# Splitting TensorE products: 64-row pairs in two streams, or one 128-row instruction with 64-row pairs where they remain

## The chip, the cores and the metric

The kernel runs on one core of one Trainium2 chip. The metric is the device time of one execution in microseconds (us), taken over several runs. The profiled execution is one run of the same program with the hardware profiler on; its instruction times are what the views of the profile show.

Engines are named as in the profile: PE is TensorE (PEld is its weight load), DVE is VectorE, ACT is ScalarE, POOL is GpSimd, SP is the engine that issues most transfers.

## What is computed

There are 33,280 tokens (8 batches of 4,160) of 192 features. A short causal convolution with 7 taps comes first, whose weights are a softmax per token and head (8 heads of 24 features); then a layer that takes the largest of three linear maps to 768 hidden features, and one linear map back to 192:

```python
w = softmax(weight_gen, axis=-1)                      # b, s, 8 heads, 7 taps
x = einsum("bshk,bskhg->bshg", w, windows_of(x_pad))  # 33280 x 192
h = maximum(maximum(x @ w1, x @ w2), x @ w3)          # 33280 x 768
out = h @ w_out                                       # 33280 x 192
```

The kernel computes h as x @ w1 plus the larger of zero, x @ (w2 - w1) and x @ (w3 - w1). The x @ w1 @ w_out part needs no hidden layer at all: w1 @ w_out is composed once into a 192 x 192 matrix (tiles `wca` and `wcb`). So there are two hidden products for each of 768 hidden features, `i` = 0 and 1.

Every product is made in the format F32R, and float32 accuracy is reached by splitting each operand into a high part (rounded to F32R) and a low part (the rest): hi·hi + lo·hi + hi·lo.

## The kernel before, in words

The tokens are cut into 65 chunks (`c`) of 512 tokens, each of 4 blocks (`t`) of 128. For each chunk:

- `taps` multiplies by the 7 taps on POOL (line 370, one instruction per block) and sums on DVE (line 382).
- `blocks` turns the result so that features lie on partitions: for the first two chunks on PE (lines 402 and 403), afterwards by a transpose on DVE (line 421) and 24 small copies on ACT (line 432). 192 features are 128 (`a`) and 64 more (`b`).
- `parts` makes the splits: `xa_hi` (ACT, line 444) and `xa_lo` (line 460) of the 128, and of the last 64 the tiles `xc` (the hi, on both halves of the 128 rows, line 449) and `xb` (the lo, on one half of the rows, line 465).
- `up` (line 826) makes the hidden products of one group of 128 hidden features (`j` = 0 to 5) and one `i`, into one of 8 PSUM banks; `SLOT[512]` is the planner's cost of one. ACT then takes the ReLU of `i` = 0 (line 859), DVE the maximum with `i` = 1 (line 867), ACT rounds to `h_hi` (line 871), and DVE or, for `j` = 1 and 4, POOL makes `h_lo` (line 878).
- `down` (line 887) makes the output of one block from `h_hi`, `h_lo`, the chunk's split features, `wo` (hi and lo of w_out beside each other, 2 x 192 columns) and `wca`, `wcb`. ACT and DVE add the two halves of the columns (lines 928 and 935), and SP stores.

All products go through `products` (line 792, the matmul itself is line 802). It makes each product as two instructions of 64 rows: the lower half of the rows ("L") and the upper half ("U"), which are two tiles of the array. The two halves of one product sum into the same bank, so the upper half's first instruction waits until the lower half's last has ended; an instruction of SP that does nothing (line 808) carries that wait. While the upper half of one bank runs, the lower half of the next one does. Of one bank of `up`, the halves hold 4 or 5 products each: `xa_hi`·`wa_hi`, `xa_lo`·`wa_hi`, (`xb` or `xc`)·`wb_hi`, `xa_hi`·`wa_lo`, and in the half named `odd` also `xc`·`wb_lo`. So one `up` is 9 instructions of 64 rows and 512 columns. One `down` is 15 of each half: per half 7 or 8 of 384 columns and 8 or 7 of 192.

Per chunk these are 12 x 9 + 4 x 30 = 228 instructions of 64 rows.

The order of the instructions on each engine is found ahead of the run by a planner (class `Plan`): every piece of work is a task with a cost, an engine, its predecessors, a due time, and the buffers that it holds. The lists "L" and "U" are kept in the order in which the program adds them; the other engines take, of what is ready in the plan, the task with the earliest due time. The order in which tasks start in the plan is the order in which they are emitted. In the list of PE, the four `down` of chunk c - 1 stand in chunk c before `j` = `DOWN_AT` = 3.

Between the `up` of chunk 0 and chunk 1, `turn_weights` (lines 731 and 733) transposes w1 on PE: for each j one F32 transpose of 128 rows and two of 64 rows. `compose` (line 750) then makes `wca` and `wcb` by F32 products on all 128 rows.

Of the kernel before, what the change touches and what calls it, by code (L numbers as in the profile page):

```python
# [10 lines left out]
F32 = mybir.dt.float32  # L11
# [29 lines left out]
class Plan:  # L41
# [3 lines left out]
    FIXED = ("L", "U")  # L45
    LATENCY = 0.12

    def __init__(self, pools):
        self.free = dict(pools)
        self.waiting = {"L": [], "U": []}  # L50
        self.tasks = []
# [79 lines left out]
def lightconv_maxout_kernel(  # L131
# [30 lines left out]
    DOWN_AT = 3  # L162
# [71 lines left out]
    def hold(name):  # L234
        return Hold(name)
# [7 lines left out]
    def pin(ins):  # L243
        tc.keep_in_program_order(ins)
        return ins
# [4 lines left out]
    def act(n):  # L250
        return 0.18 + 0.00084 * n
# [138 lines left out]
    def blocks(c, ha, sums, wait):  # L390
# [3 lines left out]
        if c < ON_TENSOR:  # L394
            ba, bb = hold("bank"), hold("bank")
            got = []
            for t in range(TC):
                to = slice(t * P, (t + 1) * P)

                def turn(t=t, to=to):  # L400
                    acc = buf(ha)
                    pin(nc.tensor.transpose(buf(ba)[:, to], acc[:, t, :P], ident))
                    pin(nc.tensor.transpose(buf(bb)[:DB, to], acc[:, t, P:], ident))

                got.append(plan.add("L", 0.6, turn, [sums[t], *wait], due, [ba, bb, ha], end=0.9))
            return [ba, bb], lambda: (buf(ba), buf(bb)[:DB]), got
# [30 lines left out]
    def parts(c, hs, places, got):  # L437
# [18 lines left out]
        near = halves[0] if c < ON_TENSOR else halves[low]  # L456
# [6 lines left out]
        def b_low():  # L463
            pin(
                eng.tensor_tensor(  # L465
                    buf(b)[halves[low]], places()[1], buf(k)[near].bitcast(F32), op=ALU.subtract
                )
            )
# [255 lines left out]
    def turn_weights(j):  # L724
# [10 lines left out]
        got = plan.add("L", 0.5, turn, [one_a[jp], one_b[jp], made, *u_last()], 0, [hb], end=0.8)  # L735
# [6 lines left out]
    def compose():  # L742
        for n, (to, at) in enumerate(((wca, 0), (wcb, P))):
# [12 lines left out]
            got = plan.add("L", 2.4, mult, deps + u_last(), 0, [hb, hw1t], end=2.8)  # L756
# [19 lines left out]
    SLOT = {CH: (0.2275, 0.386), 2 * D: (0.166, 0.358), D: (0.12, 0.247)}  # L776
    uppers = []
    last_upper = []

    def u_last():  # L780
        return last_upper[-1:]

    def after(ins, other):
        tc.add_manual_dep(
            ins.ins,
            other.ins.name,
            mybir.DependencyInfo(mybir.DependencyClass.Sync, mybir.DependencyReason.DATA),
            reason="the two halves of the rows don't write to a bank together",
        )
        return ins  # L790

    def products(hb, terms_of):

        begun, before = {}, []
        for half in range(2):
            h = halves[half]
            terms = terms_of(half)
            for q, (n, w, v, deps, holds) in enumerate(terms):
                first, last = q == 0, q == len(terms) - 1

                def emit(n=n, w=w, v=v, h=h, half=half, first=first, last=last):
                    ins = nc.tensor.matmul(  # L802
                        buf(hb)[:, :n], w()[h], v()[h],
                        start=half == 0 and first, stop=half == 1 and last,
                    )
                    pin(ins)
                    if half == 0 and last:
                        begun[0] = pin(after(nc.sync.nop(), ins))
                    elif half == 1 and first:
                        after(ins, begun[0])  # L810

                slot, end = SLOT[n]
                t = plan.add(
                    "LU"[half], slot, emit, [*deps, *(before if first else [])], 0,
                    [hb, *holds], end=end,
                )
            if half == 0:
                before = [plan.add("SYNC", 0.0, lambda: None, [t], 0, [], end=0.3)]
            else:
                last_upper.append(t)  # L820
        return t
# [4 lines left out]
    def up(c, j, i):  # L826
        jp, odd = divmod(j, 2)
        (ah, al, b, k), (hi, lo, bl, cs) = parts_of[c]
        low = 1 - c % 2
        hb = hold("bank")  # L830

        def terms(half):
            got = [
                (CH, lambda: wa_hi[:, j, i], lambda: buf(ah), [w_hi[jp, i], hi], [ah]),
                (CH, lambda: wa_hi[:, j, i], lambda: buf(al), [w_hi[jp, i], lo], [al]),
                (
                    (CH, lambda: wb_hi[:, j, i], lambda: buf(b), [*b_hi[j], bl], [b])
                    if half == low
                    else (CH, lambda: wb_hi[:, j, i], lambda: buf(k), [*b_hi[j], *cs], [k])
                ),  # L840
                (CH, lambda: wa_lo[:, j, i], lambda: buf(ah), [w_lo[jp, i], hi], [ah]),
            ]
            if half == odd:
                got.append((CH, lambda: wb_lo[:, jp, i], lambda: buf(k), [b_lo[jp], *cs], [k]))
            return got

        made = products(hb, terms)
        clock[0] += 4.5 * SLOT[CH][0]
# [38 lines left out]
    def down(c, t):  # L887
# [7 lines left out]
        def terms(half):  # L895
            got = [
                (2 * D, lambda: buf(ah)[:, sl], lambda: wca, first, [ah]),
                (D, lambda: buf(al)[:, sl], lambda: wca[:, :D], first, [al]),
                (
                    (D, lambda: buf(b)[:, sl], lambda: wcb[:, :D], first, [b])  # L900
                    if half == low
                    else (2 * D, lambda: buf(k)[:, sl], lambda: wcb, first, [k])
                ),
            ]
            for j in range(NJ):
                got.append(
                    (
                        2 * D, lambda j=j: buf(hh)[:, j, sl], lambda j=j: wo[:, j],
                        [his[j], o_hi[j], o_lo[j]], [hh],
                    )  # L910
                )
                got.append(
                    (
                        D, lambda j=j: buf(hl)[:, j, sl], lambda j=j: wo[:, j, :D],
                        [los[j]], [hl],
                    )
                )
            return got

        made = products(hb, terms)  # L920
        clock[0] += 7 * (SLOT[2 * D][0] + SLOT[D][0]) + 0.14
# [52 lines left out]
    for c in range(ON_TENSOR, NC):  # L974
        pass
    for c in range(NC):
        if c < ON_TENSOR:
            tokens(c)
        for j in range(NJ):
            if c > 0 and j == DOWN_AT and c < NC - 1:  # L980
# [4 lines left out]
            for i in range(NI):  # L985
                up(c, j, i)
# [45 lines left out]
```

## Time and profile before

| | us |
|---|---|
| median of 3 runs | 1443.07 |
| lowest, highest | 1436.2, 1443.39 |
| the profiled execution, its own time | 1444.6 |
| its span (first to last instruction) | 1442.8 |
| PE busy | 1402.0 |
| ACT, POOL, DVE busy | 1117.3, 1104.2, 1043.4 |
| mean granted clock of PE | 0.987 |

The span is what the views of the profile divide up. A matmul's row has its start and its modelled end: matmuls are pipelined, and neighbours overlap. So the pace is read from the starts, not from the lengths. In the timeline, neighbouring instructions of one kind are merged in one row with their count (x2), from the first one's start to the last one's end. A shape such as 64*128 64x512 is the weights' rows and columns, then the rows and columns of what streams past them.

### The profile page before, as it was taken

The page shows a single profiled execution, that of the slowest core. Times are in us where ns is not written, and L with a number is a line of the kernel's source. Part 1 is how long each engine was busy: PE and PEld are TensorE (multiplying, and loading weights), DVE is VectorE, ACT ScalarE, POOL GpSimd, SP SyncE. Part 2 cuts the span into 40 slices and gives each one's busy share as a digit, 9 for nine tenths or more (in the row PEclk, how much of TensorE's full clock was granted, in tenths as well). Part 3 has the DMA queues.
Part 4 walks back from the last instruction along what each step waited for, and adds up shares of the span by engine and source line. Part 5 has one row for each costly group of instructions (what it writes and reads, how often), then busy time and mean ns, then how long its engine had stood idle before and what let it go on. Part 6 is the DMA issues. An engine that isn't in the chain of part 4 may idle for free.

```text
span 1442.8 us, 37119 instructions
## 1 busy us (share of the span) xinstructions
PE 1402.0 (97%) x14878; PEld 1366.1 (95%) x14878; DVE 1043.4 (72%) x1433; ACT 1117.3 (77%) x2828; POOL 1104.2 (77%) x609
## 2 busy tenths in 40 slices
PE   2889999999999999999999999999999999999999
PEld 1579999999999999999999999999999999999998
DVE  7867777777777787777778777877877677777543
ACT  3547878878877887787788778877888887788773
POOL 6769888778877887887788778778877877787421
PEclk9679999999999999999999999999999999999999
DMA  7102111111111111111011111101111111110000
GB/s 249 46 1 79 57 68 57 68 68 57 68 46 46 57 68 68 68 57 64 28 57 68 68 68 57 68 25 67 57 68 68 57 68 44 48 57 24 23 21 26
DMA packets 23405, 85.08 MB, mean 59 GB/s; under 512 B 2768, under 2 KB 9544, under 8 KB 19136
## 3 DMA queue, kind: packets, MB, share of 16 engines
q1 hardware_dynamic: 23112, 82.44, 15.5%
q8 instruction: 116, 1.90, 0.5%
q14 instruction: 57, 0.47, 0.1%
q10 hardware_dynamic: 120, 0.28, 0.1%
HBM read 57.15 MB, written 25.56 MB: 57 GB/s over the span
## 4 chain that ended last, share of the span: by engine, by line
PE 95%; POOL 1%; DMA 1%; ACT 1%; SPq 1%; DVE 1%; issue 0%; POOLq 0%
PE bank L802 95%; POOL r L370 1%; DMA xt<-in_x_dram 1%; SPq L532 1%; DVE den L344 0%; ACT room L432 0%; DMA raw<-in_moe_w_dram 0%; SPq L516 0%; PE bank L733 0%; ACT m L859 0%; POOL wa_lo L643 0%; PE bank L731 0%; ACT wb_hi L684 0%; DVE acc L382 0%; ACT bank L573 0%
## 5 line engine op out<-in xcount | busy, mean ns | idle before, releaser
L370 POOL TENSOR_TENSOR r<-xt,wt 128x1344 f32<-128x1344 f32 x260 | 727.1, 2845 | 143.2 <-DVE acc L382 142.9
L802 PE MATMUL bank<-wo,h_hi 64*128 64x384 f32 x3120 | 675.0, 357 | 0.0
L802 PE MATMUL bank<-wo,h_lo 64*128 64x192 f32 x3120 | 603.4, 249 | 0.0
L432 ACT COPY room<-room 32x128 f32<-32x128 f32 x1512 | 448.4, 297 | 79.0 <-DVE room L421 55.9
L802 PEld LDWEIGHTS bank<-wo,h_lo 64*128 64x128 f32 x3120 | 493.0, 188 | 0.0
L802 PEld LDWEIGHTS bank<-wo,h_hi 64*128 64x128 f32 x3120 | 489.2, 186 | 0.0
L802 PE MATMUL bank<-xa_hi,wa_hi 64*128 64x512 f32 x1560 | 479.9, 394 | 6.0 <-ACT wa_hi L637 3.4
L802 PE MATMUL bank<-xa_hi,wa_lo 64*128 64x512 f32 x1560 | 477.9, 390 | 3.4 <-POOL wa_lo L643 3.3
L802 PE MATMUL bank<-xa_lo,wa_hi 64*128 64x512 f32 x1560 | 476.8, 391 | 0.5 <-DVE xa_lo L460 0.5
L382 DVE TENSOR_REDUCE acc<-r 128x192 f32<-128x1344 f32 x260 | 399.8, 1538 | 0.6 <-POOL r L370 0.3
L859 ACT ACTIVATE m<-bank 128x512 f32<-128x512 f32 x390 | 234.5, 601 | 71.4 <-PE bank L802 66.7
L935 DVE TENSOR_TENSOR o<-bank,ob 128x192 f32<-128x192 f32 x260 | 92.4, 356 | 268.7 <-ACT ob L928 268.5
L802 PE MATMUL bank<-xb,wb_hi 64*128 64x512 f32 x780 | 284.5, 390 | 0.3 <-DVE xb L465 0.3
L802 PE MATMUL bank<-xc,wb_hi 64*128 64x512 f32 x780 | 281.1, 390 | 0.2 <-ACT wb_hi L684 0.2
L802 PEld LDWEIGHTS bank<-xa_hi,wa_hi 64*128 64x128 f32 x1560 | 255.3, 186 | 13.5 <-ACT wa_hi L637 4.3
L802 PEld LDWEIGHTS bank<-xa_hi,wa_lo 64*128 64x128 f32 x1560 | 255.3, 186 | 11.2 <-POOL wa_lo L643 5.6
L802 PEld LDWEIGHTS bank<-xa_lo,wa_hi 64*128 64x128 f32 x1560 | 254.9, 187 | 6.4 <-DVE xa_lo L460 1.5
L802 PE MATMUL bank<-xc,wb_lo 64*128 64x512 f32 x780 | 258.0, 389 | 0.0
L867 DVE TENSOR_TENSOR bank<-bank,m 128x512 f32<-128x512 f32 x260 | 179.0, 689 | 42.2 <-PE bank L802 24.3
L878 POOL TENSOR_TENSOR h_lo<-m,h_hi 128x512 fp32r<-128x512 f32 x130 | 171.7, 1321 | 40.0 <-ACT h_hi L871 39.9
L802 PE MATMUL bank<-wca,xa_hi 64*128 64x384 f32 x520 | 183.4, 353 | 0.0
L878 DVE TENSOR_TENSOR h_lo<-bank,h_hi 128x512 fp32r<-128x512 f32 x260 | 172.4, 681 | 11.4 <-ACT h_hi L871 11.2
(79 smaller groups left out, 2012.5 us busy)
## 6 DMA issues: line engine op xcount, KB each, us to landing
xt<-in_x_dram SPq DMA_DIRECT2D x31, 1344.0 KB, 5.8
out_dram<-o SPq DMA_DIRECT2D x64, 384.0 KB, 2.3
wt<-in_weight_gen_dram SPq DMA_DIRECT2D x32, 224.0 KB, 2.6
h_hi<-in_moe_w_dram SPq DMA_DIRECT2D x6, 256.0 KB, 2.9
xt<-in_x_dram SPq DMA_DIRECT2D x1, 1152.0 KB, 5.8
h_lo<-in_moe_w_dram SPq DMA_DIRECT2D x6, 128.0 KB, 4.0
raw<-in_moe_w_dram SPq DMA_DIRECT2D x3, 256.0 KB, 3.6
room<-in_moe_w_out_dram SPq DMA_DIRECT2D x2, 384.0 KB, 6.4
```

The source lines that it names most:

```text
L370: nc.gpsimd.tensor_tensor(buf(hr).rearrange("p (h g) k -> p k h g", g=G), buf(hx)[:, la + t : la + t + K].rearrange("p k (h g) -> p k h g" ...
L382: pin(nc.vector.tensor_reduce(buf(ha)[:, t], buf(hr), axis=AX.X, op=ALU.add))
L432: pin(nc.scalar.copy(to[:, :, p : p + 32], b[p : p + 32, :, f : f + 32]))
L532: nc.sync.dma_start(out=raw_b()[h, jps[0] : jps[-1] + 1, i].rearrange("p j n w -> p j (n w)"), in_=w[P:].rearrange("p (j o n) -> p j o n", ...
L802: ins = nc.tensor.matmul(buf(hb)[:, :n], w()[h], v()[h], start=half == 0 and first, stop=half == 1 and last,)
L859: lambda: pin(nc.scalar.activation(buf(hm), buf(hb), AF.Relu)), [made], due,
L867: lambda: pin(nc.vector.tensor_tensor(buf(keep), buf(hb), buf(hm), op=ALU.max)),
L878: eng.tensor_tensor(buf(hl)[:, j], buf(keep), buf(hh)[:, j].bitcast(F32), op=ALU.subtract)
L935: nc.vector.tensor_tensor(buf(ho)[:, t], buf(hb)[:, :D], buf(hq), op=ALU.add)
```

## The change

All products whose operands lie on 128 rows become one instruction of 128 rows. The two lists "L" and "U" become one, "T", in one order, and the instructions on SP that carried the wait from half to half are gone.

- **The splits of the last 64 features.** `xb` now holds the lo on one half of the rows and the hi on the other, so `xb`·`wb_hi` on 128 rows gives both lo·hi and hi·hi. `xc` holds the hi on the half in which `xb` has the lo. The copies are as many as before and as large; one of the two goes to `xb`.
- **`up`** is now called for a pair of groups (`jp`, hidden groups 2jp and 2jp + 1), with four banks. For each bank 4 instructions of 128 rows and 512 columns (`up_full`), and for each `i` one pair of 64 rows (`up_half`): hi·`wb_lo`, the even group on the lower half of the rows and the odd group on the upper half, into two banks. The order in a pair of groups: `up_full` for the two banks of `i` = 0, `up_half` for `i` = 0, `up_half` for `i` = 1 (which begins the two banks of `i` = 1), `up_full` for the two banks of `i` = 1.
- **`down`** is one list of 16 products for each block: 7 of 384 and 9 of 192 columns. All are on 128 rows but the fourth, hi of the last features with the low part of `wcb`, which is one instruction of 64 rows and 192 columns.
- The four `down` of chunk c - 1 stand ahead of pair 1 of chunk c (`DOWN_AT` = 1 of 3), so after 2 groups of 6 and not after 3.
- The planner's costs: one of 512 columns 0.2165 (0.2275 before), of 384 columns 0.163 (0.166), of 192 columns 0.114 (0.12), a pair of `up_half` 0.228.

Per chunk these are 12 x 4 + 6 x 2 + 4 x 16 = 124 instructions on PE.

```diff
-    FIXED = ("L", "U")
+    FIXED = ("T",)
...
-    DOWN_AT = 3
+    DOWN_AT = 1
...
             plan.add(
-                "ACT", act(CH), lambda h=h: pin(nc.scalar.copy(buf(k)[h], places()[1])), of_b,
-                due - 2.5, [k, *hs],
-            )
-            for h in halves
+                "ACT", act(CH),
+                lambda odd=odd: pin(
+                    nc.scalar.copy(buf(k if odd == low else b)[halves[odd]], places()[1])
+                ),
+                of_b, due - 2.5, [k if odd == low else b, *hs],
+            )
+            for odd in range(2)
...
-        bl = plan.add(name, cost, b_low, cs, due - 1.4, [b, k, *hs])
+        bl = [plan.add(name, cost, b_low, cs, due - 1.4, [b, k, *hs]), *cs]
...
-    SLOT = {CH: (0.2275, 0.386), 2 * D: (0.166, 0.358), D: (0.12, 0.247)}
+    SLOT = {CH: (0.2165, 0.386), 2 * D: (0.163, 0.358), D: (0.114, 0.247)}
...
-                    ins = nc.tensor.matmul(
-                        buf(hb)[:, :n], w()[h], v()[h],
-                        start=half == 0 and first, stop=half == 1 and last,
-                    )
-                    pin(ins)
-                    if half == 0 and last:
-                        begun[0] = pin(after(nc.sync.nop(), ins))
-                    elif half == 1 and first:
-                        after(ins, begun[0])
...
+    def product_of(hb, n, w, v, deps, holds, first, last):
+        def emit():
+            pin(nc.tensor.matmul(buf(hb)[:, :n], w(), v(), start=first, stop=last))
+
+        slot, end = SLOT[n]
+        t = plan.add("T", slot, emit, deps, 0, [hb, *holds], end=end)
+        last_product[:] = [t]
         return t
...
+    def up_full(c, j, i, hb, first, last):
+        jp = j // 2
+        (ah, al, b, k), (hi, lo, bl, cs) = parts_of[c]
+        terms = [
+            (lambda: wa_hi[:, j, i], lambda: buf(ah), [w_hi[jp, i], hi], ah),
+            (lambda: wa_hi[:, j, i], lambda: buf(al), [w_hi[jp, i], lo], al),
+            (lambda: wb_hi[:, j, i], lambda: buf(b), [*b_hi[j], *bl], b),
+            (lambda: wa_lo[:, j, i], lambda: buf(ah), [w_lo[jp, i], hi], ah),
+        ]
+        for q, (w, v, deps, h) in enumerate(terms):
+            t = product_of(hb, CH, w, v, deps, [h], first and q == 0, last and q == 3)
...
+    def up_half(c, jp, i, banks, first):
...
+            for odd, h in enumerate(halves):
+                pin(
+                    nc.tensor.matmul(
+                        buf(banks[odd]), wb_lo[h, jp, i], buf(k if odd == low else b)[h],
+                        start=first, stop=not first,
+                    )
+                )
+
+        t = plan.add("T", 0.228, emit, [b_lo[jp], *cs], 0, [*banks, b, k], end=0.42)
...
+    def up(c, jp):
+        banks = {(odd, i): hold("bank") for i in range(NI) for odd in range(2)}
+        of = lambda i: [banks[0, i], banks[1, i]]
+        for odd in range(2):
+            up_full(c, 2 * jp + odd, 0, banks[odd, 0], True, False)
+        t = up_half(c, jp, 0, of(0), False)
+        for odd in range(2):
+            rest(c, 2 * jp + odd, 0, banks[odd, 0], t)
+        up_half(c, jp, 1, of(1), True)
+        for odd in range(2):
+            t = up_full(c, 2 * jp + odd, 1, banks[odd, 1], False, True)
+            rest(c, 2 * jp + odd, 1, banks[odd, 1], t)
...
+        near = halves[1 - low]
+        terms = [
+            (2 * D, lambda: buf(ah)[:, sl], lambda: wca, first, [ah]),
+            (D, lambda: buf(al)[:, sl], lambda: wca[:, :D], first, [al]),
+            (D, lambda: buf(b)[:, sl], lambda: wcb[:, :D], first, [b]),
+            (D, lambda: buf(b)[near, sl], lambda: wcb[near, D:], first, [b]),
+        ]
+        for j in range(NJ):
...
+        for q, (n, w, v, deps, holds) in enumerate(terms):
+            made = product_of(hb, n, w, v, deps, holds, q == 0, q == len(terms) - 1)
```

`rest` is what followed the products in `up` before (ReLU, maximum, `h_hi`, `h_lo`), unchanged.

More of the change, by code (lines that the diff above doesn't have):

```diff
@@ L455, in parts @@
         eng = nc.vector if c < ON_TENSOR else nc.gpsimd
-        near = halves[0] if c < ON_TENSOR else halves[low]
+        near = 0 if c < ON_TENSOR else low
         def a_low():
@@ L465, in b_low @@
                 eng.tensor_tensor(
-                    buf(b)[halves[low]], places()[1], buf(k)[near].bitcast(F32), op=ALU.subtract
+                    buf(b)[halves[low]], places()[1],
+                    buf(k if near == low else b)[halves[near]].bitcast(F32), op=ALU.subtract,
                 )
@@ L754, in mult @@
                     )
-            got = plan.add("L", 2.4, mult, deps + u_last(), 0, [hb, hw1t], end=2.8)
+            got = plan.add("T", 2.4, mult, deps + u_last(), 0, [hb, hw1t], end=2.8)
             hi = plan.add(
@@ L773, in compose @@
             )
-    SLOT = {CH: (0.2275, 0.386), 2 * D: (0.166, 0.358), D: (0.12, 0.247)}
-    uppers = []
-    last_upper = []
+    SLOT = {CH: (0.2165, 0.386), 2 * D: (0.163, 0.358), D: (0.114, 0.247)}
+    last_product = []
     def u_last():
[L781 to L788, printed above, removed]
-        )
[L790 to L802, printed above, removed]
-                        buf(hb)[:, :n], w()[h], v()[h],
-                        start=half == 0 and first, stop=half == 1 and last,
-                    )
-                    pin(ins)
-                    if half == 0 and last:
-                        begun[0] = pin(after(nc.sync.nop(), ins))
-                    elif half == 1 and first:
-                        after(ins, begun[0])
[L812 to L820, printed above, removed]
+        return last_product[-1:]
+    def product_of(hb, n, w, v, deps, holds, first, last):
[4 more added lines that the diff above has]
+        last_product[:] = [t]
         return t
@@ L828, in up @@
+    def up_half(c, jp, i, banks, first):
         (ah, al, b, k), (hi, lo, bl, cs) = parts_of[c]
         low = 1 - c % 2
[L830 to L845, printed above, removed]
@@ L847, in up, with emit @@
-        made = products(hb, terms)
-        clock[0] += 4.5 * SLOT[CH][0]
+        def emit():
+            for odd, h in enumerate(halves):
[6 more added lines that the diff above has]
+        t = plan.add("T", 0.228, emit, [b_lo[jp], *cs], 0, [*banks, b, k], end=0.42)
+        clock[0] += 0.228
@@ L849, in up, with rest @@
+    def rest(c, j, i, hb, made):
         due = clock[0] + 1
@@ L893, in down @@
         first = of_c if c == 0 else []
[L895 to L898, printed above, removed]
-                (
[L900 to L910, printed above, removed]
-                )
[L912 to L916, printed above, removed]
-                )
-            return got
-        made = products(hb, terms)
-        clock[0] += 7 * (SLOT[2 * D][0] + SLOT[D][0]) + 0.14
+        near = halves[1 - low]
[6 more added lines that the diff above has]
+        for j in range(NJ):
+            terms.append(
+                (
+                    2 * D, lambda j=j: buf(hh)[:, j, sl], lambda j=j: wo[:, j],
+                    [his[j], o_hi[j], o_lo[j]], [hh],
+                )
+            )
+            terms.append(
+                (
+                    D, lambda j=j: buf(hl)[:, j, sl], lambda j=j: wo[:, j, :D], [los[j]], [hl],
+                )
+            )
+        for q, (n, w, v, deps, holds) in enumerate(terms):
+            made = product_of(hb, n, w, v, deps, holds, q == 0, q == len(terms) - 1)
+            clock[0] += SLOT[n][0]
         due = clock[0] + 1.5
@@ L978, in lightconv_maxout_kernel @@
             tokens(c)
-        for j in range(NJ):
-            if c > 0 and j == DOWN_AT and c < NC - 1:
+        for jp in range(NP):
+            if c > 0 and jp == DOWN_AT and c < NC - 1:
                 if c == 1:
@@ L984, in lightconv_maxout_kernel @@
                     down(c - 1, t)
-            for i in range(NI):
-                up(c, j, i)
+            up(c, jp)
         if c == 0:
```

14 lines of the change are left out of this document (7 added, 7 removed).

## The prediction

> **What bounds the kernel now.** I read the page first: busy times, then the chain of waits that ended last.
>
> ```profile
> span 1442.8 us, 37119 instructions
> ...
> PE 1402.0 (97%) x14878; PEld 1366.1 (95%) x14878; DVE 1043.4 (72%) x1433; ACT 1117.3 (77%) x2828; POOL 1104.2 (77%) x609
> ...
> PE 95%; POOL 1%; DMA 1%; ACT 1%; SPq 1%; DVE 1%; issue 0%; POOLq 0%
> ```
>
> The end is set by PE alone: 95% of the chain is PE. A change of the list of PE is worth just what it does to PE's pace. To get that pace I asked for the busy time in one stretch, 200 to 1400 us, clear of start and end.
>
> ```profile
> core 0: us, PE busy (x) PEld busy (x) DVE busy (x) ACT busy (x) POOL busy (x), PEclk, DMA share, GB/s
> 200.00:1400.00 1200.00, 1200.00 (x13113) 1184.10 (x13111) 881.66 (x1192) 984.16 (x2504) 937.67 (x503) 1.00 0.15 55
> ```
>
> 13113 products in 1200 us at the full granted clock, 228 of them per chunk (12 x 9 and 4 x 30 by the code): one chunk takes 228 x 1200 / 13113 = 20.86 us. Per chunk ACT is busy 82% of that, POOL 78%, DVE 73%; none is close behind PE.
>
> Then the timeline of PE, in the middle of the run, where two streams of 64 rows run, and at 64 us, where one half runs by itself:
>
> ```profile
> 700.39 0.42 PE L802 MATMUL bank<-xa_hi,wa_hi 64*128 64x512 f32 x2
> 700.62 0.42 PE L802 MATMUL bank<-xa_lo,wa_hi 64*128 64x512 f32 x2
> ```
>
> ```profile
> 63.89 0.39 PE L802 MATMUL bank<-xa_lo,wa_hi 64*128 64x512 f32 x1
> 64.11 0.39 PE L802 MATMUL bank<-xb,wb_hi 64*128 64x512 f32 x1
> 64.34 0.39 PE L802 MATMUL bank<-xa_hi,wa_lo 64*128 64x512 f32 x1
> 64.57 0.39 PE L802 MATMUL bank<-xc,wb_lo 64*128 64x512 f32 x1
> 64.88 0.33 PE L731 MATMUL bank<-ident,w1a 128*128 128x128 f32 x1
> 65.15 0.33 PE L733 MATMUL bank<-ident,b 64*128 64x64 f32 x2
> 65.41 0.33 PE L731 MATMUL bank<-ident,w1a 128*128 128x128 f32 x1
> ```
>
> A half alone takes (64.57 - 63.89) / 3 = 0.227 us for 512 columns. Two halves take the same 0.23 for both, and the second ends 0.42 - 0.39 = 0.03 after the first. So the two tiles really run side by side. The 12 `up` of a chunk are 54 such pairs, 12.29 us (with the 0.2275 that the planner also has). What is left, 8.57, is four `down`, 2.14 each.
>
> The last four rows are the heart of the forecast, and I come back to them: they are the only place in this run where PE goes back and forth between instructions of 64 rows and of 128.
>
> **The change, first without any price for going back and forth.** Full-row F32R products do not occur in this trace, so their pace must come from neighbours. `compose` is a stream of full-row F32 instructions:
>
> ```profile
> 82.06 0.39 PE L802 MATMUL bank<-xa_hi,wa_lo 64*128 64x512 f32 x1
> 82.37 4.17 PE L750 MATMUL bank<-wo,raw 128*128 128x192 f32 x24
> 86.47 0.44 PE L802 MATMUL bank<-wca,xa_hi 64*128 64x384 f32 x1
> 86.75 0.25 PE L802 MATMUL bank<-wca,xa_lo 64*128 64x192 f32 x1
> ```
>
> ```profile
> L750 PE MATMUL bank<-wo,raw 128*128 128x192 f32 x24 | 4.2, 330 | 0.0
> ```
>
> From first start to last start are 4.17 - 0.33 = 3.84 us, 23 steps: 0.167, or 0.163 if the first step holds a load of 0.1 that nothing hides. 192 columns of F32 go as long as 384 of F32R or nearly (a 64-row half needs 0.20 for 384 below), so I take 0.163 for 384 columns and 0.163 x 512 / 384 = 0.217 for 512; the upper bound is the half's own 0.2275. For 192 columns the end of the run helps, where one half of one `down` runs alone, first PE, then its weight loads:
>
> ```profile
> 1438.12 0.36 PE L802 MATMUL bank<-wo,h_hi 64*128 64x384 f32 x1
> 1438.32 0.25 PE L802 MATMUL bank<-wo,h_lo 64*128 64x192 f32 x1
> 1438.40 0.36 PE L802 MATMUL bank<-wo,h_hi 64*128 64x384 f32 x1
> ```
>
> ```profile
> 1438.03 0.18 PEld L802 LDWEIGHTS bank<-wo,h_hi 64*128 64x128 f32 x1
> 1438.14 0.19 PEld L802 LDWEIGHTS bank<-wo,h_lo 64*128 64x128 f32 x1
> 1438.32 0.18 PEld L802 LDWEIGHTS bank<-wo,h_hi 64*128 64x128 f32 x1
> ```
>
> 384 columns step 0.20, 192 columns 0.08 to 0.09, together 0.28; loads come no closer than 0.11. Behind a 192-column product the next load is the longer thing, so I take 0.11 for 192 columns at 128 rows. Bounds: 0.0875, the half's own step, and 0.125, which would bring the pair of 384 and 192 back to today's 0.2875.
>
> The Trainium skill, "TensorE: Matmul & The Clock Gate", section "Back-to-back issue gap", gives an isolated warm product as columns / 2.4 plus 2.5 ns, which is an estimate of 0.0825 for 192 columns; by it the whole sum would be 36 x 0.0275 x 64 = 63 us lower. The loads 0.11 apart speak for my value, and the page itself says that the formula leaves out the load budget at few columns.
>
> Per chunk then: `up` 48 x 0.217 = 10.42; six pairs of halves x 0.2275 = 1.37, and 3 x 0.03 for the second tile's lag = 0.09: 11.88, against 12.29. `down` 4 x (7 x 0.163 + 9 x 0.11) = 8.52, against 8.57. Together 20.40: a gain of 0.46 per chunk. `up` gains 0.01 on each product; `down` gains nothing, because the hi·lo term of the last features, which rode in one half's instruction before, is now an instruction of its own.
>
> **The price of changing the number of rows.** In the rows around 64.57: the last 64-row product of 512 columns starts, and the full-row transpose after it starts 0.31 later, not 0.227: 0.08 over. The same at 82.06 to 82.37. It is not the load of data: the row of loads says so, and shows more.
>
> ```profile
> 64.88 0.14 PEld L731 LDWEIGHTS bank<-ident,w1a 128*128 128x128 f32 x1 [0.35 <-issue]
> 65.14 0.20 PEld L733 LDWEIGHTS bank<-ident,b 64*128 64x128 f32 x2
> 65.41 0.14 PEld L731 LDWEIGHTS bank<-ident,w1a 128*128 128x128 f32 x1
> ```
>
> At one shape the next load starts with the product before it (1438.32 in both lists above) and hides under it. At a change of rows it doesn't: the load of L731 starts at 64.88, with its own product, 0.31 after the product before it. "issue" says that no semaphore released it. So PE emptied first, and then loaded with nothing to hide the load. That adds the 0.11 of a load; the first product after the change at 86.47 is the check, 0.28 to its successor where 384 columns step 0.20, 0.08 more. One change from half to full rows costs 0.08 + 0.11 = 0.19. From full to half I take the same emptying, 0.08, and 0.08 to 0.11 for the load: 0.16 to 0.19. I take 0.185 for both. A lower bound comes from the transposes: one round (64.88 to 65.41) is one full and two half instructions, 0.53 with two changes. Transposes of one row count follow each other so:
>
> ```profile
> 69.15 0.42 PE L403 MATMUL bank<-ident,acc 128*64 128x128 f32 x1
> 69.36 0.42 PE L402 MATMUL bank<-ident,acc 128*128 128x128 f32 x1
> ```
>
> ```profile
> 68.40:70.50 2.10, 2.02 (x10) 1.40 (x8) 2.10 (x3) 0.63 (x2) 0.63 (x1) 0.50 0.00 0
> ```
>
> 0.21 each at a granted clock of 0.50, so 0.105 at the full clock at which the round ran (an estimate). Three would be 0.32, and the two changes cost at least (0.53 - 0.32) / 2 = 0.105 each. Here the weights' columns change (128*64, 128*128) and nothing is lost; it is the rows that matter. Upper bound 0.20, a whole load and 0.09 of emptying.
>
> The Trainium skill, "TensorEngine Tiling (Array Packing)", section "Key Properties", says that changing the tiling mode, not merely the tile, drains TensorE. It gives no price. By that rule the change pays at every passage below; this trace agrees, with 0.31 where 0.227 would do.
>
> How often: in a pair of hidden groups, all eight full products of `i` = 0, then both pairs of halves together, then the eight of `i` = 1: two passages, 6 per chunk. In each `down` the fourth product is 64 rows between full ones: two passages, 8 per chunk. 14 x 0.185 = 2.59 us per chunk. None of it lies beside other work, since PE is the chain.
>
> **The other edits.** The SP instructions between the halves vanish, but the whole run waited for them only
>
> ```profile
> PEld bank L802 <- SPq L808: 1.4, 2, 0.8
> ```
>
> 1.4 us in two places: nothing. The copies that make `xb` and `xc` are as many and as large. One list in place of two means that a product that waits holds all behind it: `down` of chunk c - 1 now comes 2 groups (4.3 us) after the last hidden product, where it was 3 (6.1), and needs the last `h_hi`, `h_lo` 1.9 us into its first block.
>
> ```profile
> L370 POOL TENSOR_TENSOR r<-xt,wt 128x1344 f32<-128x1344 f32 x260 | 727.1, 2845 | 143.2 <-DVE acc L382 142.9
> ...
> L867 DVE TENSOR_TENSOR bank<-bank,m 128x512 f32<-128x512 f32 x260 | 179.0, 689 | 42.2 <-PE bank L802 24.3 <-ACT m L859 9.3 <-ACT h_hi L871 1.4
> L878 POOL TENSOR_TENSOR h_lo<-m,h_hi 128x512 fp32r<-128x512 f32 x130 | 171.7, 1321 | 40.0 <-ACT h_hi L871 39.9
> ...
> L871 ACT CAST h_hi<-bank 128x512 fp32r<-128x512 f32 x260 | 146.2, 585 | 8.0 <-DVE bank L867 5.6
> ```
>
> The longest is group 4, through POOL: 0.69 + 0.59 + 1.32, and up to 2.85 behind a tap product, 5.45 us. Cover is 0.9 (group 5) + 4.3 + 1.6 = 6.8 us, so I cost it at nothing; without that cover each us late is 64 us. Banks: at most six of eight are held at once.
>
> **The sum.** 20.40 + 2.59 = 22.99 per chunk, 2.13 more than 20.86. I count 64 of 65 chunks, as the first waits for weights anyway. 64 x 2.13 = 136 us: the profiled execution's 1444.6 becomes 1581. It lies 1.5 above the median, so against the median I say **1579 us**, 9% slower.
>
> **The rivals.**
>
> *A change of rows costs nothing between F32R products.* All rows above have F32 on one side of the passage, so it could be the change of format, or of transposing, that empties PE. Against it: L731 and L733 are both F32 transposes, and they empty PE in every round. Then 20.40 per chunk, 64 x 0.46 = 29 us less: 1414, faster. It decides from a price under 0.46 / 14 = 0.033 us per passage. Chance 0.10.
>
> *The lone 64-row product of `down` goes as a full-row instruction would*, and only `up` pays: 6 x 0.185 - 0.46 = 0.65, 42 us more: 1485. Against it: L733 shows the same 0.26 from L731 for either half. Chance 0.05.
>
> *`down` waits for the last `h_lo` as well* as paying for the passages: 1 us per chunk takes 1579 to 1643. It needs a queue on POOL or DVE longer than 6.8 us. Chance 0.03.
>
> *The change doesn't do what it says:* the two halves of a pair run one after the other: 6 x 0.2275 - 0.09 = 1.28 more per chunk, 1661. The 0.03 between the halves' ends today speaks against it. Chance 0.02.
>
> **How the numbers follow.** My forecast has 0.80. Its bounds: a price of 0.105 gives 1507, of 0.20 gives 1592; 192 columns at 0.0875 give 1527, at 0.125 give 1614; 512 columns at 0.2275 give 1611. So 1505 to 1615, which leaves out the rivals, 0.20. A measurement can tell about 0.5%, 7 us, from no change (the three runs lie within 7.2). Slower by more than that: 0.80 + 0.05 + 0.03 + 0.02 = 0.90. Of the rival without a price, 0.01 is for a price close to the point of no change, and 0.09 is faster.
>
> **What the profile after would show.** About 8,060 products on line 802's successors. Full products of 512 columns start 0.217 apart, of 384 and 192 together 0.27. At each passage the load starts 0.1 after the last column of the product before it, with "issue" as its releaser: some 900 such gaps on PEld, whose busy share drops. From the load before the fourth product of a `down` to the fifth's, 0.28 (0.11 without a price). One chunk takes 23.0 us. I would be wrong if loads of 64 rows start together with the full product before them, if a chunk takes 20.4, or if PE's gaps are waits for DVE, ACT or POOL.

## The result, and the profile after

| | us |
|---|---|
| before, median of 4 runs | 1441.37 |
| after, median of 4 runs (1616.26 to 1618.77) | 1617.8 |
| ratio, 95% interval | 1.1229 (1.1196 to 1.1263) |
| span of the profiled execution, before and after | 1442.8, 1616.2 |

The kernel became 12% slower. The page of the changed kernel first: still PE alone, and its weight loads, which were busy 95% of the span, now 78%.

```profile
span 1616.2 us, 22601 instructions
...
PE 1578.0 (98%) x8118; PEld 1260.9 (78%) x8118; DVE 1051.4 (65%) x1433; ACT 1123.0 (69%) x2828; POOL 1108.3 (69%) x609
...
PE 96%; POOL 1%; DMA 1%; SPq 1%; ACT 1%; DVE 0%; issue 0%; POOLq 0%; DVEq 0%
```

The same stretch as before, 200 to 1400 us, and the two longest entries of PE's list of waits that lie outside the start (us in total, times, longest):

```profile
200.00:1400.00 1200.00, 1200.00 (x6252) 964.78 (x6252) 791.83 (x1056) 867.43 (x2195) 849.11 (x453) 1.00 0.14 52
```

```profile
PEld bank L788 <- issue: 71.6, 197, 0.7
PEld bank L820 <- issue: 70.2, 195, 0.7
```

One chunk takes 124 x 1200 / 6252 = 23.80 us at the full granted clock, where it took 20.86. PE waits for none of DVE, ACT and POOL in the steady part (busy 1200 of 1200 us); what its loads wait for is "issue", and the list has 392 long waits, two for each of the 195 visits to 64 rows in the hidden products and two more. At the changes of row count in `down` the loads stand idle for only 0.10 us each, which the list leaves out: in the trace from 200 to 1400 us there are 300 gaps of 0.36 and 406 of 0.10, together 14 per chunk, as forecast.

The timeline of PE around one such visit, and the loads beside it:

```profile
713.06 0.40 PE L788 MATMUL bank<-xb,wb_hi 128*128 128x512 f32 x1
713.29 0.39 PE L788 MATMUL bank<-xa_hi,wa_lo 128*128 128x512 f32 x1
713.61 0.50 PE L820 MATMUL bank<-xc,wb_lo 64*128 64x512 f32 x1
713.62 0.49 PE L820 MATMUL bank<-xb,wb_lo 64*128 64x512 f32 x1
713.95 0.39 PE L820 MATMUL bank<-xc,wb_lo 64*128 64x512 f32 x1
713.95 0.39 PE L820 MATMUL bank<-xb,wb_lo 64*128 64x512 f32 x1
714.27 0.50 PE L788 MATMUL bank<-xa_hi,wa_hi 128*128 128x512 f32 x1
714.61 0.39 PE L788 MATMUL bank<-xa_lo,wa_hi 128*128 128x512 f32 x1
714.84 0.39 PE L788 MATMUL bank<-xb,wb_hi 128*128 128x512 f32 x1
```

```profile
713.06 0.19 PEld L788 LDWEIGHTS bank<-xa_hi,wa_lo 128*128 128x128 f32 x1
713.61 0.18 PEld L820 LDWEIGHTS bank<-xc,wb_lo 64*128 64x128 f32 x1 [0.36 <-issue]
...
714.27 0.19 PEld L788 LDWEIGHTS bank<-xa_hi,wa_hi 128*128 128x128 f32 x1 [0.36 <-issue]
714.38 0.19 PEld L788 LDWEIGHTS bank<-xa_lo,wa_hi 128*128 128x128 f32 x1
714.61 0.19 PEld L788 LDWEIGHTS bank<-xb,wb_hi 128*128 128x128 f32 x1
```

Read the starts. Where the row count stays, full products step 0.23 (713.06 to 713.29, 714.61 to 714.84). At a change the step is 0.32 (713.29 to 713.61, 713.95 to 714.27), and the first product behind it steps 0.34 (713.61 to 713.95, 714.27 to 714.61), because its own load starts only with it (714.27) and the load of the next product stands behind that (714.38). With 0.227 for the usual step, one change costs 0.093 + 0.113, about 0.205 us. Both products of a pair start within 0.01 of each other, so the tiles do lie beside each other.

And one block of `down`, where the fourth product has 64 rows (the row x2 holds the third and the fourth):

```profile
703.97 0.36 PE L788 MATMUL bank<-wca,xa_hi 128*128 128x384 f32 x1
704.17 0.25 PE L788 MATMUL bank<-wca,xa_lo 128*128 128x192 f32 x1
704.25 0.56 PE L788 MATMUL bank<-wcb,xb 128*128 128x192 f32 x2
704.74 0.44 PE L788 MATMUL bank<-wo,h_hi 128*128 128x384 f32 x1
705.02 0.25 PE L788 MATMUL bank<-wo,h_lo 128*128 128x192 f32 x1
705.11 0.36 PE L788 MATMUL bank<-wo,h_hi 128*128 128x384 f32 x1
705.30 0.25 PE L788 MATMUL bank<-wo,h_lo 128*128 128x192 f32 x1
705.39 0.36 PE L788 MATMUL bank<-wo,h_hi 128*128 128x384 f32 x1
...
706.53 0.36 PE L788 MATMUL bank<-wca,xa_hi 128*128 128x384 f32 x1
```

The third and fourth together take 704.25 to 704.74, 0.49. A block takes 706.53 - 703.97 = 2.56, where it was 2.14. And a pair of 384 and 192 columns takes more than I gave it, though nothing changes rows there: from one 384 to the next, 0.28 to 0.29 (705.11 to 705.39), as in one half before.

### The profile page after: what moved, and what is told of

Same layout as the page of the kernel before. It is cut to its first block, busy times and chain, and to the rows that moved or that the text cites. A ratio compares the mean times of both kernels' runs of the same rounds, so it can differ in the third digit from the quotient of the medians.

```text
span 1616.2 us, 22601 instructions
## 1 busy us (share of the span) xinstructions
PE 1578.0 (98%) x8118; PEld 1260.9 (78%) x8118; DVE 1051.4 (65%) x1433; ACT 1123.0 (69%) x2828; POOL 1108.3 (69%) x609
## 4 chain that ended last, share of the span: by engine, by line
PE 96%; POOL 1%; DMA 1%; SPq 1%; ACT 1%; DVE 0%; issue 0%; POOLq 0%; DVEq 0%
PE bank L788 88%; PE bank L820 8%; POOL r L370 1%; DMA xt<-in_x_dram 1%; SPq L536 0%; ACT room L432 0%; DMA raw<-in_moe_w_dram 0%; PE bank L737 0%; SPq L520 0%; PE bank L735 0%; POOL wa_lo L647 0%; ACT h_hi L867 0%; POOL h_lo L874 0%; POOL wx L635 0%; PE bank L402 0%
## 5 line engine op out<-in xcount | busy, mean ns | idle before, releaser
L788 PE MATMUL bank<-wo,h_hi 128*128 128x384 f32 x1560 | 487.9, 375 | 0.0
L788 PE MATMUL bank<-wo,h_lo 128*128 128x192 f32 x1560 | 391.9, 251 | 0.0
L788 PE MATMUL bank<-xa_hi,wa_hi 128*128 128x512 f32 x780 | 329.3, 422 | 5.1 <-ACT wa_hi L641 3.6
L788 PEld LDWEIGHTS bank<-wo,h_hi 128*128 128x128 f32 x1560 | 293.6, 188 | 26.0 <-issue 0.2
L788 PE MATMUL bank<-xb,wb_hi 128*128 128x512 f32 x780 | 307.9, 395 | 1.8 <-DVE xb L468 1.0
L788 PE MATMUL bank<-xa_hi,wa_lo 128*128 128x512 f32 x780 | 307.1, 394 | 1.9 <-POOL wa_lo L647 1.8
L788 PE MATMUL bank<-xa_lo,wa_hi 128*128 128x512 f32 x780 | 307.4, 394 | 0.5 <-DVE xa_lo L463 0.5
L788 PEld LDWEIGHTS bank<-wo,h_lo 128*128 128x128 f32 x1560 | 298.9, 192 | 0.0
L867 ACT CAST h_hi<-bank 128x512 fp32r<-128x512 f32 x260 | 152.1, 585 | 50.7 <-DVE bank L863 44.1
L788 PEld LDWEIGHTS bank<-xa_hi,wa_lo 128*128 128x128 f32 x780 | 147.7, 189 | 34.9 <-POOL wa_lo L647 2.8
```

Source lines behind the costliest of these rows:

```text
L788: pin(nc.tensor.matmul(buf(hb)[:, :n], w(), v(), start=first, stop=last))
L867: "ACT", act(CH), lambda: pin(nc.scalar.copy(buf(hh)[:, j], buf(keep))), [m], due + 1,
```

## The experiments

Theory A is the forecast's: changes of the row count cost about 0.2 us each. The rivals stand in the expectations.

### The downs on full rows

```diff
-            (D, lambda: buf(b)[near, sl], lambda: wcb[near, D:], first, [b]),
+            (D, lambda: buf(b)[:, sl], lambda: wcb[:, D:], first, [b]),
```

> The changed kernel with one edit: the fourth product of each down runs on all 128 rows (it adds the lo times lo of the last 64 features, which is harmless), so the 8 changes of row count per chunk in the downs are gone and the 6 in the hidden products stay. Theory A (a change of row count costs about 0.2 us each, by the changed kernel's own steps of 0.32 and 0.34 where 0.2275 is usual): one block falls from 2.56 to 6 x 0.2865 + 0.20 + 0.085 + 0.115 + 0.11 = 2.23 us, so 0.33 x 4 x 64 = 84 us less than 1618: about 1533. Rival B (the downs are slower because the hi-lo term is an instruction of its own and full rows are no faster than half rows; the change of rows is nearly free): no more than 10 us less, over 1605. Rival C (a lone product of 64 rows is handled as a full one and only the hidden products pay): no change, 1618.

Measured: 1534.37 us (1533.61 to 1535.57), ratio to before 1.0644 (1.0601 to 1.0687). That is 83 us less than the changed kernel, where theory A said 84. Rivals B and C fall: the same number of instructions, one of each block's on 128 rows and not on 64, and the time of eight changes per chunk is gone. Per change it is 83 / 64 / 8 = 0.163 us; less than in the hidden products, probably because beside a product of 192 columns part of the load stands out without a change too (argued, not tested).

### The pairs of halves apart

```diff
-        up_half(c, jp, 1, of(1), True)
         for odd in range(2):
-            t = up_full(c, 2 * jp + odd, 1, banks[odd, 1], False, True)
+            up_full(c, 2 * jp + odd, 1, banks[odd, 1], True, False)
+        t = up_half(c, jp, 1, of(1), False)
+        for odd in range(2):
             rest(c, 2 * jp + odd, 1, banks[odd, 1], t)
```

> The changed kernel with the two pairs of 64-row products of a group pair no longer beside each other: the pair for i = 1 comes at the end of its banks, so 12 changes of row count per chunk in the hidden products where there were 6. The same instructions otherwise. Theory A: one visit to 64 rows costs 0.41 us more than the same steps without a change; three more visits per chunk: 3 x 0.41 x 64 = 79 us more, about 1697. Rival B (changes of rows nearly free): 1618 within 10.

Measured: 1697.61 us (1697.46 to 1697.75), 79.8 more than the changed kernel; theory A said 79. Same instructions, six more changes per chunk: 79.8 / 64 / 6 = 0.208 us each, as the steps of 0.32 and 0.34 say. The list of waits agrees: the "issue" waits ahead of the halves' loads (the first row) double from 195 to 389.

```profile
PEld bank L820 <- issue: 138.0, 389, 0.7
PEld bank L788 <- issue: 70.9, 289, 0.4
```

### No 64-row product at all

```diff
-    wb_lo = const.tile([P, NP, NI, P], F32R, name="wb_lo")
+    wb_lo = const.tile([P, NJ, NI, P], F32R, name="wb_lo")
...
             (lambda: wa_lo[:, j, i], lambda: buf(ah), [w_lo[jp, i], hi], ah),
+            (lambda: wb_lo[:, j, i], lambda: buf(b), [*b_lo[j], *bl], b),
         ]
```

(with the first experiment's edit, the weights' lo copied to both halves by four more copies on ACT for each pair of groups, and `up` without `up_half`.)

> The changed kernel with no 64-row product at all: the down edit of the first kernel, and the weights' lo of the last 64 features laid out on both halves of the rows, so that each hidden bank gets a fifth full product (it adds lo times lo) in place of half a pair. No change of row count is left in the steady part. Theory A with a full-row pace of 0.2275 to 0.23 per 512 columns: a group pair is 20 x 0.228 = 4.56 us against 4.49 measured with two visits' worth of pairs, so 0.07 x 3 x 64 = 13 us more than the first kernel: about 1546. Against 1441 for the kernel with two 64-row streams this shows what the packing of halves is worth. Rival D (changes of rows cost more than the steps beside them show, by waits further on): clearly less than the first kernel, under 1515.

Measured: 1574.78 us (1573.02 to 1576.25), 29 over theory A's number, and rival D is out too, since it wanted less. The reason stands in neither theory: PE now waits, in a place that neither had. Its list of waits:

```profile
PEld bank L797 <- ACT m L839: 34.5, 22, 1.7
PE bank L797 <- ACT m L839: 25.2, 22, 1.3
```

The waits begin at 850 us and come once per chunk, the first four for an `h_lo` of POOL, the others, from 964 us on, for the ReLU: a bank is still held, because the ReLU on ACT stands behind the copies of the next chunk's features. In the trace the step between two products goes up to 1.7 us there; over the run these steps hold 34 us beyond usual ones.

### The same with the planner's period

```diff
-    PERIOD = 21.0
+    PERIOD = 21.7
```

> The third kernel (no 64-row product) came out at 1575, 29 over its expectation, and its trace shows PE waiting 1.0 to 1.7 us in each chunk from 850 us on, for the ReLU on ACT, behind the small copies of the next chunk. One edit: the planner's period, by which due times of the next chunk's features are set, is 21.7 in place of 21.0, the planner's own cost of a chunk of this kernel (60 x 0.2165 + 8.67). Theory K (the due times of the next chunk's copies run ahead by 0.66 us per chunk, until the planner puts them before the ReLU; the products themselves cost what was expected): the waits go and the time is about 1541. Rival L (five banks' products in a row leave ACT too little room whatever the due times): the waits stay, 1570 or more.

Measured: 1537.16 us (1536.52 to 1539.02), ratio to before 1.0658 (1.0639 to 1.0676). Theory K holds: the waits of PE for the ReLU are gone from the list, and 37.6 us with them (theory K had 1541). So without any change of rows the kernel takes 1537, against 1534 with six per chunk. In the hidden products the six changes are nearly paid back by the pairs: 12 more full products (12 x 0.227 = 2.72 us) take about what 6 pairs and 6 changes take (6 x 0.2275 + 6 x 0.205 = 2.60).

### Products by themselves

After the last `down` 24 products in a row of each kind, which nobody reads:

```diff
...
+    def full(o, r, n, s, e):
+        return nc.tensor.matmul(o, w(r), buf(xa)[:, :n], start=s, stop=e)
+    def half(o, r, n, s, e):
+        return nc.tensor.matmul(o, w(r)[:DB], buf(xa)[:DB, :n], start=s, stop=e)
+    def plain(o, r, n, s, e):
+        return nc.tensor.matmul(o, w1a[:, r % 6], buf(xa).bitcast(F32)[:, :n], start=s, stop=e)
+    def turns(o, r, n, s, e):
+        return (half if r % 2 else full)(o, r, n, s, e)
```

> The changed kernel with products appended after its last down, 24 in a row of each kind, whose results nobody reads: F32R on 128 rows, F32R on 64 rows, F32 on 128 rows, each with 512, 384, 256, 192 and 128 columns; then 128 and 64 rows in turns with 512, 384 and 192 columns. The time of the run is not compared, the steps in the trace are. Theory E (an F32R product has a fixed cost of some 14 ns beside columns / 2.4 GHz, at 128 rows as at 64): steps of 0.2275, 0.174, 0.121 us at 512, 384, 256 columns. Rival F (an F32R column takes 0.444 ns, a slower rate): 0.2275, 0.171, 0.114. In both, 192 and 128 columns stop at the load, 0.11. Rival G (full-row F32R alone goes at columns / 2.4 and the 0.2275 in the kernel is contention with other engines): 0.216 at 512. F32 is expected at 2 x 0.1625 for a product of 192. In turns, theory A: 512 and 512 columns 0.32 + 0.11 each way, about 0.43 per product and 0.86 per round of two; 192 and 192 columns about 0.29 per product.

The view of one source line in the stretch of one size each. The columns: count, the length of one in ns (least, median, greatest), first and last start in us, shape. F32R on 128 rows (512, 384, 256, 192 columns):

```profile
L999 PE MATMUL bank<-xa_hi,wa_hi x23: 387/389/414, 1614.2 to 1619.2; 128*128 128x512 f32 x23
```

```profile
L999 PE MATMUL bank<-xa_hi,wa_hi x23: 333/334/346, 1619.7 to 1623.5; 128*128 128x384 f32 x23
```

```profile
L999 PE MATMUL bank<-xa_hi,wa_hi x22: 278/283/283, 1623.9 to 1626.4; 128*128 128x256 f32 x22
```

```profile
L999 PE MATMUL bank<-xa_hi,wa_hi x23: 254/273/278, 1626.8 to 1629.2; 128*128 128x192 f32 x23
```

F32R on 64 rows (512) and F32 on 128 rows (192; two instructions for each product):

```profile
L1002 PE MATMUL bank<-xa_hi,wa_hi x21: 386/386/386, 1632.5 to 1637.0; 64*128 64x512 f32 x21
```

```profile
L1005 PE MATMUL bank<-xa_hi,w1a x47: 326/326/326, 1700.0 to 1707.5; 128*128 128x192 f32 x47
```

Last start less first, by the number of steps: 5.0 / 22 = 0.227, 3.8 / 22 = 0.173, 2.5 / 21 = 0.119 and 2.4 / 22 = 0.109 us; on 64 rows 4.5 / 20 = 0.225; F32 7.5 / 46 = 0.163. (The starts are printed to 0.1; the single ones in the trace have medians of 0.2270, 0.1735, 0.1200, 0.1110, and 0.2270 on 64 rows.) But for one instruction each of ACT and DVE (0.3 us) no other engine works here, so rival G is out: it is not contention. From 512 to 384 to 256 columns the step falls by 0.0535 each: 0.418 ns per column, and what is left is 0.2270 - 512 x 0.418 = 0.013 us. Theory E holds and rival F, with 0.114 at 256 columns, falls: an F32R product costs its columns and 13 ns, on 128 rows as on 64, and the step does not go below 0.111 (192 and 128 columns), the distance at which loads follow each other. Whether the 13 ns lie in the product or in its load isn't separated, since each product here has a load of its own. F32 at 192 columns twice over, so 384 columns' worth, takes 0.163, and F32R at 384 takes 0.173: the F32 stream, from which I took the pace, lacks most of that fixed cost.

The last part, full and half in turns at 512 columns:

```profile
1713.51 0.50 PE L1002 MATMUL bank<-xa_hi,wa_hi 64*128 64x512 f32 x1
1713.94 0.50 PE L999 MATMUL bank<-xa_hi,wa_hi 128*128 128x512 f32 x1
1714.37 0.50 PE L1002 MATMUL bank<-xa_hi,wa_hi 64*128 64x512 f32 x1
...
1717.95 0.79 PE L1002 MATMUL bank<-xa_hi,wa_hi 64*128 64x512 f32 x1
1718.67 0.79 PE L999 MATMUL bank<-xa_hi,wa_hi 128*128 128x512 f32 x1
```

0.43 where 0.227 would do: 0.203 per change, in F32R on both sides, in both directions, with no engine beside PE. After 4 us the step becomes 0.72; the last section comes back to that. The turns of 192 columns, for which 0.29 was expected, ran after that, at half the clock (0.457), and so can't decide it.

### The kernel before in the changed kernel's order, and with its earlier downs

In the changed kernel the first `down` passes its wait 13 us earlier, at 79 us and not at 92. About 2 of these only mean that one group of hidden products less stands ahead of it. These two kernels ask whether the gain can be had with the two streams of before.

```diff
-    DOWN_AT = 3
+    DOWN_AT = 1
...
-        for j in range(NJ):
+        for jp in range(NP):
...
             for i in range(NI):
-                up(c, j, i)
+                for odd in range(2):
+                    up(c, 2 * jp + odd, i)
```

> The kernel before, with its two 64-row streams, but in the order of the changed kernel: for each pair of hidden groups first both banks of i = 0, then both of i = 1, and the downs after two groups of six. It asks where the 14 us come from that the changed kernel gains at its start (the first chunk's hidden products end at 57 us and not at 65, the first down passes its wait at 79 us and not at 92). Theory H (the order: weights of i = 1 are needed later, and the composed matrix is waited for less): 8 to 14 us less than before, about 1431, faster than both kernels. Rival I (the number of instructions: at the start PE runs at half clock and waits for weights, and two halves that run one after the other there take twice what one full product takes): the order gives nothing, 1442 within 4.

Measured: 1517.93 us (1514.13 to 1523.0), ratio 1.0522 (1.0501 to 1.0543): slower by 75. Half of theory H showed: the first `down` passes its wait at 81 and not at 92. Then it loses that many times over to waits that neither theory had: PE waits 22 us in 28 places for an `h_lo` of POOL.

The second has only `DOWN_AT = 2`, which is two groups of six:

> The kernel before with one edit: the downs of the chunk before stand after two groups of six, not three. Everything else as before. If theory H holds by the earlier downs alone, some 5 us less; if by the order of the banks, no change. Rival J (the last h_lo of the chunk before comes too late for the first down, 4.1 us after its products): waits of PE on POOL or DVE show in every chunk, and each 0.1 us of them costs 6 us.

Measured: 1514.37 us (1513.33 to 1518.51), ratio 1.0502 (1.0483 to 1.0521). Rival J: PE waits in the downs, in the timeline and in the list of waits, though in 29 places, about every second chunk, and not in every one.

```profile
868.71 0.39 PE L802 MATMUL bank<-xa_hi,wa_lo 64*128 64x512 f32 x1
869.39 0.44 PE L802 MATMUL bank<-wo,h_hi 64*128 64x384 f32 x1 [0.29 <-ACT h_hi L871]
869.40 0.49 PE L802 MATMUL bank<-xc,wb_lo 64*128 64x512 f32 x1
870.54 0.35 PE L802 MATMUL bank<-wo,h_lo 64*128 64x192 f32 x1 [0.65 <-DVE h_lo L878]
```

```profile
PE bank L802 <- DVE h_lo L878: 19.0, 29, 0.8
```

The first down meets the last `h_hi` and `h_lo` too early. While the lower half waits, the upper half runs dry as well, and the loss is more than the 19 and 7 us that the list shows: from one chunk's first `down` to the next's it is now 21.37 and 22.76 us in turns, where it was 20.73 and some 21.05, so 2.35 more in two chunks. That the halves then run one after the other for a while is argued from the rows above. Five times in the profiled execution the clock also fell to 0.50 for 3.4 us behind such a wait, and that chunk took 1.6 us longer still. So earlier downs alone cost 72 us in the kernel before, and the order of the banks is not to blame.

### The start's gain without the earlier downs

```diff
+        one_by_one = [(j, i) for j in range(NJ) for i in range(NI)]
+        by_pairs = [(2 * jp + odd, i) for jp in range(NP) for i in range(NI) for odd in range(2)]
+        for n, (j, i) in enumerate(by_pairs if c < 1 else one_by_one):
+            if c > 0 and n == (NI * DOWN_AT) and c < NC - 1:
...
+            up(c, j, i)
```

> The kernel before; only chunk 0's hidden products go in the changed kernel's order (both banks of i = 0 of a pair of groups, then both of i = 1), all other chunks and all downs as before, after three groups. In the kernel with pair order and earlier downs throughout, the first down's composed matrix was met at 81 us and not at 92, but PE then waited 1.2 us in every second chunk for h_lo; here those waits cannot come, since the steady part is that of before. Theory H (the start's gain is the order's): the first down passes its wait 6 to 11 us earlier and the run takes about 1434. Rival M (the gain at the start is from the earlier downs of chunk 1 alone): within 3 us of before.

Measured: 1433.0 us (1431.88 to 1437.17, 12 runs) against 1441.8 (17 runs), ratio 0.995 (0.9937 to 0.9964). The wait of the first `down`:

```profile
85.27 0.44 PE L802 MATMUL bank<-wcb,xc 64*128 64x384 f32 x1 [2.82 <-DVE wcb L767]
```

It was 92.22 with 5.22 of waiting. Theory H holds and rival M falls: the order of chunk 0 alone brings 7 us here, and 9 in the time.

The same with chunk 1 as well (`c < 2`, and the downs of chunk 1 after two groups):

> As the kernel with the order of chunk 0 changed, and chunk 1 as well: pair order, with the composition and the first four downs after two groups; from chunk 2 on as before. Theory H: 9 to 12 us less than before, about 1432, as the first down then passes its wait near 81 us. Rival M expects this one to gain and the one with chunk 0 alone not. A third outcome: the waits for h_lo begin here too (the chunk after the earlier downs has its features' tiles freed earlier but the planner's later choices shift), and the time is above 1443.

Measured: 1432.05 us (1431.07 to 1437.99, 6 runs), ratio 0.9946 (0.9925 to 0.9968). The first `down` passes its wait at 80.3, but one group less stands ahead of it (2 us), and the list of waits has a new one of 3.9 us. Between the last two kernels nothing can be told apart. Both beat the kernel before by half a per cent and the changed one by 11%.

## Why the prediction was wrong

The direction and the mechanism were right, and so, in sum, was the price. The number was 1579 and the range ended at 1615; 1617.8 came out. What failed is one term, the pace of full-row products; a second, the gain at the start, is not in the sum at all.

**Wrong: "I take 0.163 for 384 columns and 0.163 x 512 / 384 = 0.217 for 512".** Measured 0.227 to 0.23 in the kernel and 0.227 alone. I took the pace from F32 products on 128 rows, same row count but another format, and held the 64-row F32R half, 0.2275, for an upper bound. It was the value. The fixed 13 ns go with the F32R format, not with the half. So `up` gains nothing by full rows: 4.49 + 4.52 for two group pairs (714.27, 718.76 and 723.28 in the timeline), 13.5 per chunk, less six changes at 0.205 is 12.27, and 12.29 was before. And the same 13 ns make 384 columns 0.1735 in place of 0.163, while 192 columns alone are 0.111, as I took them. The pair of the two is then 0.285 in place of my 0.273, as the half's pair at the end of the old trace, 0.28, already showed, so that one `down` without a change of rows is 2.22 to 2.25 (in the trace of the first experiment), where I had 2.13 and the kernel before has 2.14.

**Right: "14 x 0.185 = 2.59 us per chunk".** The experiments give 6 x 0.205 + 8 x 0.163 = 2.53. That the sum fits so well is partly luck: one price for both kinds was 0.02 too low in the hidden products and 0.02 too high in `down`. That the formats around the passages in the old trace were F32 on one side did not matter: the changes between products by themselves, in turns, are F32R on both sides. The rival without a price falls, as does the one by which the lone 64-row product of `down` is free, and the one of pairs that run one after the other. Here the Trainium skill ("TensorEngine Tiling (Array Packing)", section "Key Properties") is borne out: a change of tiling mode drains TensorE. In this kernel that costs 0.16 to 0.21 us, the load that can't be hidden included. The estimate by "TensorE: Matmul & The Clock Gate", section "Back-to-back issue gap" (columns / 2.4 plus 2.5 ns), fits the F32 stream here, 0.163 for 384 columns' worth, but not F32R, where 512 columns measure 0.2270 and the estimate is 0.216; the measurement decides.

**Not foreseen: the start.** Per chunk 2.94 us more, times 64, would be 188; the span grew by 173.4. The first `down` passes its wait at 79 us in the changed kernel and at 92 before. In the kernel before, the order in which the first chunk asks for its weights gives 9 us by itself, an edit that I had not costed at all; that it is most of the 15 here is taken over from there, and the rest is open.

Together: pace (23.80 - 2.53 - 20.40) x 64 = 56 us more than predicted, price 4 less, start 15 less (what is left of 188): 37 of the 39 by which it missed (1617.8 - 1579).

**The range.** It listed 512 columns at 0.2275 (1611) and 192 columns at 0.125 (1614) one by one. The second stood for a pair of 384 and 192 columns as slow as in one half, 0.2875. Both were the same unknown, the fixed cost of a full-row F32R product, and came true together, the second not quite (0.285, and by the 384 columns): 1579 + 32 + 35 = 1646 was the end to name, and the gains elsewhere brought it back to 1618.

**Right, but thinner than written: the earlier downs at nothing.** In the changed kernel PE waits for no `h_hi` or `h_lo`. In the kernel before the same move costs 72 us, though the path that I added up there is the same, 5.45 us at worst, under a cover that is only some 0.2 less. There PE waits for the last group's `h_hi` on ACT and `h_lo` on DVE, while the path that I added up was that of group 4 through POOL. So that path was not what decided. That the changed kernel is spared because PE takes 23.80 per chunk where its plan says 20.43, which leaves the other engines time, is argued, not shown. That nothing had to be paid here is thus in part luck. The two kernels without any 64-row product show how such waits arise from the planner's due times alone: 37.6 us for one number.

## What to carry to other kernels

On TensorE count the changes of the row count before the columns: in this kernel each costs nearly as much as a product of 512 columns, so 64-row products belong together or are filled up to 128 rows. Of the kernels here, those that make all products as pairs of 64 rows remain the fastest, 1432 to 1443 with the `down` where they were: 54 pairs make the hidden products of a chunk, for which full rows take 60 instructions of the same pace. With full rows throughout it is 1537. Take the pace of a new kind of instruction from the row that shares its format, even if the shape differs, and when two bounds rest on one unknown, move them together. An order that suits the start can be had for the first chunk alone, without touching the steady part.

## What the runs showed of the hardware that I had not expected

The granted clock fell while PE was never without work. The stretch of products in turns, before and after 1717.5 us (time, busy PE and loads, the other three engines, granted clock, DMA):

```profile
1713.50:1717.30 3.80, 3.80 (x10) 1.66 (x9) 0.00 (x0) 0.00 (x0) 0.00 (x0) 1.00 0.00 0
1718.00:1726.00 8.00, 8.00 (x13) 3.19 (x12) 0.00 (x0) 0.00 (x0) 0.00 (x0) 0.50 0.00 0
```

With a change of rows between every two products columns stream about half of the time (0.214 of 0.43), and some 4 us after that began the clock went from 1.00 to 0.50 and stayed there. In the profiled execution of the changed kernel, where changes take 2.5 of 23.8 us, it stayed at 1.00 from 88 us on. So the row "busy" of PE does not say what the clock goes by.

The same run has another such fall, earlier, at 1649 us, without any change of rows: among the products of 128 columns on 64 rows. The same products on 128 rows, 20 us earlier and at the same step of 0.111, had kept the full clock:

```profile
1629.50:1632.00 2.50, 2.50 (x25) 2.50 (x24) 0.00 (x0) 0.00 (x0) 0.00 (x0) 1.00 0.00 0
1649.40:1650.30 0.90, 0.90 (x6) 0.90 (x6) 0.00 (x0) 0.00 (x0) 0.00 (x0) 0.50 0.00 0
```

In both, columns stream about half of the time (128 x 0.418 ns of 0.111 us). So that share alone may not be what counts, and the number of rows may count as well; but both stretches last under 3 us, and no run here tests it or shows where the limit lies.
